# A fused RWKV and FFN kernel: a new order list, score tiles cleared on GpSimd, the last two stores in halves, and identity products around them

## The chip, the cores and the metric

The kernel runs on one core of a Trainium2 chip. The metric is device time in microseconds (us), the median of several runs; lower is better. The five instruction streams are TensorE (PE), VectorE (DVE), ScalarE (ACT), GpSimd (POOL) and SyncE (SP, which issues the DMAs).

## The reference

```python
# rwkv5: batch 4, 8 heads, 768 steps, head dimension 48
for t in range(S):
    cur = einsum('bhd,bhe->bhde', u[None] * kt, vt)
    y[:, :, t] = einsum('bhd,bhde->bhe', rt, state + cur)
    state = w[None, :, :, None] * state + einsum('bhd,bhe->bhde', kt, vt)
# bridge to x of 3072 x 384, then
h = (x @ w1) * (x @ w2) @ w3        # w1, w2: 384 x 1024, w3: 1024 x 1024
out = h @ w_out                     # w_out: 1024 x 384
```

The four FFN weights arrive as 64-bit words and are made into 32-bit numbers on the chip; all else is float32.

## The kernel before, in words

**The two halves.** The sequence is cut into six chunks of 128 steps, and each chunk into four batches; one chunk of one batch is a *unit*, numbered 0 to 23, so units 4c to 4c+3 are chunk c. For each unit the kernel loads k, r and v, scales k and r by powers of the decay, and gets from TensorE the inner sums for the running state, the scores of the unit, and the output rows. The output rows are turned into columns of `xT`, 512 tokens a chunk. The FFN then runs over whole chunks: products of `xT` with w1 and w2, multiplied together, and a last product with `w34`, which is w3 times w_out and is made once (`fold`, line 427, eight turns of 16 TensorE instructions). From chunk 1 on, both FFN products go by seven block products in place of eight, with sums of weights and of tokens.

**The weights.** There are 32 pieces, each through one of three `raw` buffers and one of two `t` buffers: 0 to 7 are strips of w1 and w2, 8 to 15 are w_out, 16 to 31 are w3. Piece i is loaded (SP), its magnitude is taken (ACT, line 385), its sign (POOL, line 396; DVE for pieces 0 and 1), the two are joined (DVE, line 401), its low word is scaled (ACT, line 405) and added (DVE, line 408). w3 is then turned (DVE, line 422) for the fold. A load waits for its `raw` buffer, and a sign waits for its `t` buffer.

**The order.** Nothing is scheduled when the kernel is built. `ORDER` is a list of some 1,430 words that an outside planner wrote, and `listed()` calls the step of each word in turn; each engine then runs its own steps in that order and waits by semaphores for what others make. A word is a letter and its indices. Those that matter here:

- SP: `kr.n`, `v.n` load unit n; `W.i` fetches weight piece i; `y.n`, `z.n` write a turned unit to DRAM and read it back; `D.c.m.x` stores rows (x = 1: `osb_top`, 0: `osb_low`), line 855.
- PE: `T.n`, `R.n` transposes of k and r (488); `U.n` inner sums (563); `A.n`, `Au.n` scores (570, 591); `S.n`, `V.n` output rows (690, 713); `yt.n` turns them (729); `a`, `b` the products of chunk 0 (759); `F.j` the fold (427); `pa`, `pb` the products of the later chunks (922, 926); `P.c.m.x` the seven last products (817); `Z.n.b` n products of the identity with itself (958), which nothing reads.
- DVE: `k.n` scaling (441); `i.n`, `j.n` state (609 to 615); `m.n`, `mo.n` scores into the tile `AT` under a mask (621, 595); `fe.n` a guard before V (702); `N`, `H`, `Q` steps of the weights (390, 401, 408); `G` turns w3 (422); `cz.i` clears one of two `AT` tiles (598).
- ACT: `t`, `r`, `ku` copies of turned k and r (495, 499, 585); `Y.n` takes output rows for units 0 to 4 (724), DVE later (722); `yx.n` puts them in `xT` (735); `M`, `L` steps of the weights (385, 405); `l.n` takes the read-back unit (527); `c` takes a product (765).
- POOL: `p.i` the sign of piece i (396); `vp.n` copies of v (697).
- `E.c.m.x` gathers the last products into output rows (DVE, lines 839 to 851; ACT for x = 0).

The scores of units 0 to 4 are taken differently from those of the others, which is why the two `AT` tiles are cleared once in between.

**The end.** In the list before, the last output tile is chunk 5, row block 0: `P.5.0.6` on TensorE, `E.5.0.7` on VectorE, and two stores of 128 rows by 384 columns (192 KB each). Each engine then leaves the fast arm of an If by a branch (line 1055) over the other arm's code, and drains (line 1084).

Of the kernel before, what the change touches and what calls it, by code (L numbers as in the profile page):

```python
# [23 lines left out]
v.1 kr.2 uw k.1 vs.0 ka.0 Z.4.0 T.1 kb.0 T.0 t.1 v.2 U.0 N.0 t.0 R.0 kr.3 ku.0 i.0 j.0 vp.1 U.1 R.1 i.1 r.0 j.1 r.1  # L24
A.0 kr.4 Au.0 k.2 M.0 S.1 S.0 ku.1 m.0 vp.2 R.2 T.2 mo.0 W.1 t.2 H.0 A.1 W.2 r.2 Au.1 fe.0 k.3 L.0 V.0 kr.5 Y.0 m.1
R.3 T.3 ku.2 mo.1 U.2 Q.0 A.2 t.3 Au.2 i.2 r.3 v.3 m.2 yt.0 M.1 mo.2 yx.0 fe.1 ku.3 k.4 Z.3.0 A.3 W.3 V.1 p.2 N.1 R.4
Y.1 v.4 H.1 T.4 M.2 S.2 j.2 kr.6 yt.1 L.1 Au.3 fe.2 H.2 V.2 yx.1 vp.3 Y.2 m.3 a.0.0.0 mo.3 L.2 W.4 yt.2 Q.1 M.3 U.3
W.5 i.3 p.3 t.4 Q.2 b.0.0.0 r.4 v.5 yx.2 k.5 ku.4 a.0.1.0 ub x.5 vp.4 c.0.0.0 A.4 H.3 c.0.1.0 S.3 y.5 ps fe.3 M.4 p.4
u.0.0.0 j.3 L.3 d.5 V.3 W.6 Q.3 M.5 U.4 v.6 Au.4 H.4 p.5 Y.3 kr.8 m.4 yt.3 L.4 b.0.1.0 mo.4 yx.3 i.4 vp.5 a.0.0.1 H.5
W.7 cz.1 a.0.3.2 L.5 Q.4 W.8 M.6 Q.5 p.6 c.0.0.1 vs.6 k.6 b.0.2.2 c.0.3.2 z.5 x.6 H.6 u.0.1.0 M.7 p.7 b.0.4.2 e.5 f.5  # L30
M.8 y.6 h.5 kr.7 L.6 j.4 H.7 S.4 W.9 U.5 L.7 fe.4 Q.6 V.4 l.5 Q.7 p.8 W.10 cz.0 Y.4 A.5 H.8 a.0.2.2 m.5 L.8 W.11 i.5
j.5 M.9 p.9 Q.8 b.0.3.2 k.7 c.0.2.2 z.6 H.9 M.10 p.10 u.0.2.2 L.9 Q.9 a.0.4.2 H.10 u.0.3.2 L.10 W.12 p.11 M.11 Q.10
x.7 a.0.1.1 c.0.4.2 H.11 W.13 L.11 u.0.4.2 U.6 l.6 Q.11 a.0.6.2 k.8 W.14 c.0.1.1 d.6 M.12 p.12 e.6 f.6 v.7 H.12
b.0.0.1 y.7 c.0.6.2 d.7 kr.9 p.13 M.13 e.7 L.12 b.0.1.1 f.7 H.13 Q.12 A.6 M.14 u.0.0.1 p.14 b.0.6.2 L.13 W.15 i.6 vs.7
Q.13 H.14 j.6 L.14 W.16 Q.14 a.0.5.2 u.0.6.2 m.6 W.17 x.8 M.15 p.15 u.0.1.1 a.0.7.2 c.0.5.2 d.8 e.8 z.7 H.15 M.16 p.16
# [12 lines left out]
s.0.0.3 B.3 pb.1.0.3 gb.1.0.5 E.0.1.2 P.0.0.2 gb.1.0.7 pa.1.1.0 E.0.0.2 E.0.0.3 P.0.0.1 ga.1.1.0 pa.1.1.1 E.0.0.1
pa.1.1.4 ga.1.1.5 P.0.0.6 pa.1.0.2 P.0.0.5 ga.1.0.6 gb.1.0.3 pa.1.1.5 E.0.0.6 E.0.0.7 pb.1.0.7 D.0.0.1 ga.1.1.1
pb.1.0.2 gb.1.0.4 gb.1.0.8 pa.1.1.6 gb.1.0.6 pb.1.1.0 ga.1.1.3 ga.1.1.2 s.1.0.0 pa.1.1.7 s.1.0.1 P.0.1.1 ga.1.1.4  # L50
s.1.0.3 pb.1.1.4 s.1.0.2 E.0.1.1 pa.1.1.2 P.0.0.4 ga.1.1.6 pa.1.1.3 E.0.0.4 E.0.0.5 D.0.0.0 S.8 ga.1.1.7 U.10 gb.1.1.0
fe.8 V.8 k.12 l.10 pb.1.1.5 v.11 x.12 z.11 A.10 gb.1.1.1 Y.8 pb.1.1.1 gb.1.1.3 i.10 m.10 pb.1.1.2 y.12 vs.11 kr.15
gb.1.1.5 j.10 P.1.0.0 gb.1.1.6 yt.8 E.1.0.0 P.0.1.5 yx.8 g.10 U.11 P.0.1.6 k.13 f.12 P.1.1.0 d.13 e.13 kr.16 x.13
pb.1.1.7 E.1.1.0 P.0.1.3 y.13 pb.1.1.6 E.0.1.3 E.0.1.6 E.0.1.7 P.0.1.4 gb.1.1.2 D.0.1.1 gb.1.1.4 pb.1.1.3 gb.1.1.8
s.1.1.0 s.1.1.1 P.1.0.5 gb.1.1.7 s.1.1.3 P.1.0.2 s.1.1.2 E.0.1.4 E.1.0.2 P.1.0.6 E.0.1.5 D.0.1.0 P.1.0.3 P.1.1.2
E.1.0.3 E.1.0.6 P.1.0.1 E.1.1.2 P.1.0.4 E.1.0.1 E.1.0.7 D.1.0.1 P.1.1.1 E.1.0.4 E.1.0.5 D.1.0.0 P.1.1.3 E.1.1.1 S.9
E.1.1.3 P.1.1.5 fe.9 l.11 z.12 V.9 E.1.1.6 A.11 Y.9 P.1.1.4 i.11 j.11 v.12 yt.9 m.11 P.1.1.6 yx.9 E.1.1.4 g.11 E.1.1.5
D.1.1.0 S.11 E.1.1.7 S.10 D.1.1.1 fe.11 V.11 fe.10 l.12 f.13 V.10 v.14 Y.11 U.12 v.13 vs.12 k.14 A.12 z.13 yt.11
pa.2.0.0 m.12 yx.11 Y.10 ga.2.0.0 i.12 yt.10 vs.14 pa.2.0.1 j.12 yx.10 x.14 g.12 U.13 xs.2.0 y.14 xs.2.1 S.12 xs.2.2
# [48 lines left out]
def kernel(  # L108
# [46 lines left out]
    DM = H * D  # L155
# [171 lines left out]
    def body(arm, fast):  # L327
# [269 lines left out]
        def clear(i):  # L597
            nc.vector.memset(ats[i], 0.0)
# [378 lines left out]
        def plain():  # L977
# [8 lines left out]
            def seven(c):  # L986
# [3 lines left out]
                for m in range(B // 2):  # L990
# [4 lines left out]
                    for x in range(2):  # L995
                        store(c, m, x, nc.scalar)
# [92 lines left out]
```

## Time and profile before

| what | us |
|---|---|
| median of 5 runs | 494.57 |
| lowest, highest | 493.32, 497.68 |
| the profiled execution, its own time | 495.46 |
| its span from first to last instruction | 493.6 |
| PE busy in the span | 472.7 |
| DVE busy | 329.3 |
| ACT busy | 197.5 |
| POOL busy | 63.3 |

The span is 1.9 us short of the execution's own time, and that execution is 0.9 us over the median. PE is busy for 96% of the span; matmuls overlap, so that share tells where PE stood still and not how fast it worked. Queue q1 carries the data, q8 and q14 carry instructions: q8 moved 42 packets of 16 KB and q14 blocks of 8 KB.

### The profile page before, as it was taken

How to read it: one execution, taken by the hardware profiler on the slowest of the kernel's cores; microseconds unless marked ns; L12 is line 12 of the kernel's file. 1: busy time of each engine (PE TensorE's matmuls, PEld its weight loads, DVE VectorE, ACT ScalarE, POOL GpSimd, SP SyncE). 2: the span in 40 equal slices, each digit the busy share in tenths (PEclk: the TensorE clock that was granted, in tenths of full speed). 3: DMA queues.
4: the chain of work that ended last, by engine and by line, in shares of the span. 5: the costliest groups of instructions: out<-in, count | busy, mean ns of one | idle time of the engine just before them, and what ended most of it. 6: DMA issues, size and time to landing. Idle time of an engine off the chain costs nothing.

```text
span 493.6 us, 12176 instructions
## 1 busy us (share of the span) xinstructions
PE 472.7 (96%) x5070; PEld 392.7 (80%) x5070; DVE 329.3 (67%) x647; ACT 197.5 (40%) x454; POOL 63.3 (13%) x57
## 2 busy tenths in 40 slices
PE   7699899989999999999999999999999999999995
PEld 6586454656769988997888898889998889888894
DVE  5689998989999257659685993677462536316152
ACT  4776555848622124028516362422263132122200
POOL 3047544354500000000000000000000000000000
PEclk9989999999999999999999999999999999999999
DMA  8989969999830004326524550044150000100002
GB/s 190 242 215 265 215 185 237 215 231 221 226 76 34 15 20 113 97 83 161 144 65 113 131 128 18 20 118 139 64 146 1 0 3 17 49 1 0 1 1 69
DMA packets 100479, 52.72 MB, mean 107 GB/s; under 512 B 79296, under 2 KB 89792, under 8 KB 100416
## 3 DMA queue, kind: packets, MB, share of 16 engines
q1 hardware_dynamic: 99792, 51.86, 40.6%
q8 instruction: 42, 0.69, 0.6%
q14 instruction: 21, 0.17, 0.1%
q10 hardware_dynamic: 624, 0.00, 0.1%
HBM read 39.65 MB, written 12.19 MB: 105 GB/s over the span
## 4 chain that ended last, share of the span: by engine, by line
PE 75%; DVE 13%; issue 3%; DMA 3%; POOL 2%; ACT 2%; SPq 1%; ACTq 0%; DVEq 0%; POOLq 0%
PE ps_accB L922 10%; PE ps_w L427 6%; PE ps_Ab L922 4%; PE ps_accC L922 3%; PE ps_accC L926 3%; PE ps_s4b L817 3%; PE ps_accB L926 3%; PE ps_a12b L817 3%; PE ps_Aa L922 3%; PE ps_a11b L817 3%; PE ps_s3t L817 3%; PE ps_s1t L817 3%; PE ps_a22t L817 3%; PE ps_s2t L817 3%; PE ps_Fb L926 2%
## 5 line engine op out<-in xcount | busy, mean ns | idle before, releaser
L396 POOL TENSOR_SCALAR t<-raw 128x512 f32<-128x512 f32 (+2 forms) x30 | 52.5, 1752 | 61.3 <-DMA raw<-in_moe_w_dram 18.2
L922 PE MATMUL ps_accB<-sumw,w 128*128 128x256 f32 x160 | 45.9, 389 | 0.0
L427 PE MATMUL ps_w<-wo,w3T 128*128 128x384 f32 x128 | 42.7, 488 | 0.1
L427 PEld LDWEIGHTS ps_w<-wo,w3T 128*128 128x128 f32 x128 | 23.9, 190 | 15.7 <-issue 0.4
L471 ACT ACTIVATE ynat<-vnat,dg 128x48 f32<-128x48 f32 x144 | 34.4, 324 | 0.5 <-PE ps_x L729 0.4
L922 PEld LDWEIGHTS ps_accB<-sumw,w 128*128 128x128 f32 x160 | 28.9, 190 | 6.0 <-ACT u2a L939 1.1
L735 ACT COPY xT<-ps_x 128x384 f32<-128x384 f32 x24 | 11.5, 481 | 54.5 <-PE ps_x L729 54.3
L405 ACT ACTIVATE t<-raw 128x512 uint32<-128x512 uint32 (+2 forms) x32 | 22.7, 710 | 19.8 <-DVE wo L401 8.7
L527 ACT COPY kT<-tt 128x1024 f32<-128x1024 f32 x19 | 19.9, 1046 | 25.0 <-PE ps_y L690 18.7
L441 DVE TENSOR_TENSOR krs<-krin,pn_in 128x768 f32<-128x768 f32 (+1 forms) x25 | 24.1, 969 | 5.7 <-PE ps_a L563 4.1
L922 PE MATMUL ps_accC<-xT,sumw 128*128 128x256 f32 x80 | 23.8, 379 | 0.0
L926 PE MATMUL ps_accB<-xT,w 128*128 128x256 f32 x80 | 23.8, 379 | 0.0
L926 PE MATMUL ps_accC<-xT,w 128*128 128x256 f32 x80 | 23.8, 379 | 0.0
L922 PE MATMUL ps_Ab<-xT,w 128*128 128x256 f32 x80 | 22.6, 384 | 0.4 <-ACT ps_accB L937 0.4
L759 PE MATMUL ps_a<-xT,w 128*128 128x512 f32 (+1 forms) x60 | 22.2, 514 | 0.8 <-ACT xT L735 0.8
L759 PE MATMUL ps_b<-xT,w 128*128 128x512 f32 (+1 forms) x60 | 22.2, 512 | 0.5 <-DVE half L609 0.5
L922 PE MATMUL ps_Aa<-xT,w 128*128 128x256 f32 x80 | 22.3, 381 | 0.4 <-ACT ps_accB L937 0.4
L922 PE MATMUL ps_accB<-sumw,sumw 128*128 128x256 f32 x80 | 20.7, 382 | 0.0
L621 DVE COPY_PREDICATED AT<-later,ps_a 128x512 f32<-128x512 int32 x24 | 17.6, 731 | 1.8 <-PE ps_a L591 1.4
L759 PEld LDWEIGHTS ps_a<-xT,w 128*128 128x128 f32 x60 | 11.1, 190 | 9.5 <-issue 7.2
L511 DVE STREAM_TRANSPOSE tr<-krs 128x768 f32<-128x768 f32 x19 | 18.4, 969 | 0.2
L759 PEld LDWEIGHTS ps_b<-xT,w 128*128 128x128 f32 x60 | 11.1, 190 | 9.3 <-issue 7.2
(187 smaller groups left out, 1091.3 us busy)
## 6 DMA issues: line engine op xcount, KB each, us to landing
raw<-in_moe_w_dram SPq DMA_DIRECT2D x64, 128.0 KB, 3.4
scratch<-tr SPq DMA_DIRECT2D x19, 384.0 KB, 3.4
raw<-in_moe_w_dram SPq DMA_DIRECT2D x8, 768.0 KB, 5.7
tt<-scratch SPq DMA_DIRECT2D x38, 128.0 KB, 2.8
krin<-in_k_dram SPq DMA_DIRECT2D x24, 192.0 KB, 3.7
krin<-in_r_dram SPq DMA_DIRECT2D x24, 192.0 KB, 4.2
vnat<-in_v_dram SPq DMA_DIRECT2D x24, 192.0 KB, 3.3
raw<-in_moe_w_out_dram SPq DMA_DIRECT2D x32, 96.0 KB, 2.8
```

Source lines behind the costliest of these rows:

```text
L396: nc.gpsimd.tensor_scalar(part["t", i].bitcast(F32), words(i)[1].bitcast(F32), 0.0, None, ALU.mult)
L405: nc.scalar.activation(out=part["t", i], in_=words(i)[0], func=COPY, scale=2.0 ** -29)
L427: nc.tensor.matmul(ps, lhsT=w3T[j][:, kc, :], rhs=wo[kc], start=(kc == 0), stop=(kc == KF - 1))
L441: nc.vector.tensor_mul(krs[n % NS][:, which, :, :D], kr[:, which], pn[:, which, :, :D])
L471: nc.scalar.activation(out=ynat[n][:, h, :], in_=vnat[n % NV][:, h, :], func=COPY, scale=dg[n][:, h:h + 1])
L511: nc.vector.transpose(out=blocks[n].rearrange("x m e t -> x e m t"), in_=krs[n % NS][:, :, :, :D])
L527: nc.scalar.copy(out=turned(n).rearrange("x g p (z t) -> x (g p) z t", t=Q), in_=tts.rearrange("x z e t -> x e z t"))
L621: nc.vector.copy_predicated(AT[n], later.bitcast(I32)[:, None, None, :].to_broadcast([C, 2, NP, T]), upper(n))
L759: nc.tensor.matmul(ps, lhsT=(w1 if x == "a" else w2)[:, z, q, js], rhs=xT[c][:, q, ts], start=(q == 0), stop=(q == KM - 1))
L817: nc.tensor.matmul(ps, lhsT=operand(c, j // 2, a)[:, j % 2, m * C:(m + 1) * C], rhs=w34[:, KH * (x == 1) + j, :DH] if x < 2 else made[b][: ...
L922: nc.tensor.matmul(ps, lhsT=quarter(w, g, i, x), rhs=(b11, b21, b22, t4, b12, t2, t3)[x], start=x in (0, 4) and i == 0, stop=True, skip_gr ...
L926: nc.tensor.matmul(ps, lhsT=wide_of[w][:, g + half * HZ, 2, i * P:(i + 1) * P], rhs=xT[c][:, 2, side * TH:(side + 1) * TH], start=False, s ...
```

## The change

It does four things.

1. **A new list**, planned again; the header of the change says that the plan takes account of TensorE's instruction packets. The same steps are called, but for those below. Among the moves: on SP `kr.4` goes ahead of `v.2` and `kr.3`; on DVE `Q.0` goes ahead of `k.3`; on PE `Au.1` goes behind `V.0`, `T.3` behind `Au.2`, `S.4` and `V.4` behind six products, and `U.9`, `A.9`, `pa.1.0.4` and other products go behind `F.7`. The weight pieces keep their order.
2. **`cz.1` and `cz.0`** run on POOL, between `p.6` and `p.7` and between `p.13` and `p.14`.
3. **The last two stores** (now of chunk 5, row block 1) become four of 192 columns, each issued when its half is made.
4. **Identity products**: `Z.3.0` (3) becomes `Z.7.1` (7, into another pool's tile, a little later), and a new `Z.4.0` (4) stands behind the last product of all.

```diff
 ORDER = """
-v.1 kr.2 uw k.1 vs.0 ka.0 Z.4.0 T.1 kb.0 T.0 t.1 v.2 U.0 N.0 t.0 R.0 kr.3 ku.0 i.0 j.0 vp.1 U.1 R.1 i.1 r.0 j.1 r.1
-A.0 kr.4 Au.0 k.2 M.0 S.1 S.0 ku.1 m.0 vp.2 R.2 T.2 mo.0 W.1 t.2 H.0 A.1 W.2 r.2 Au.1 fe.0 k.3 L.0 V.0 kr.5 Y.0 m.1
-R.3 T.3 ku.2 mo.1 U.2 Q.0 A.2 t.3 Au.2 i.2 r.3 v.3 m.2 yt.0 M.1 mo.2 yx.0 fe.1 ku.3 k.4 Z.3.0 A.3 W.3 V.1 p.2 N.1 R.4
-Y.1 v.4 H.1 T.4 M.2 S.2 j.2 kr.6 yt.1 L.1 Au.3 fe.2 H.2 V.2 yx.1 vp.3 Y.2 m.3 a.0.0.0 mo.3 L.2 W.4 yt.2 Q.1 M.3 U.3
...
-d.11 L.28 y.10 F.5 e.11 W.31 Q.28 M.29 p.29 G.6.0 f.11 kr.12 H.29 M.30 p.30 v.10 L.29 Q.29 H.30 pa.1.0.1 z.10 X.5
-G.6.1 p.31 L.30 M.31 Q.30 F.6 ga.1.0.5 G.7.0 xs.1.0 E.0.0.0 xs.1.1 xs.1.2 kr.13 vs.10 H.31 s.0.1.0 L.31 Q.31 s.0.1.1
-xs.1.3 U.9 wa.0 X.6 A.9 wa.1 pa.1.0.4 wa.2 pa.1.0.5 G.7.1 wa.3 F.7 ga.1.0.1 wb.0 ga.1.0.3 wb.2 k.11 s.0.1.2 kr.14 i.9
...
-E.5.1.4 P.5.1.5 P.5.0.3 E.5.1.5 E.5.1.6 D.5.1.0 E.5.1.7 D.5.1.1 P.5.0.1 E.5.0.3 P.5.0.5 E.5.0.4 P.5.0.6 E.5.0.6
-E.5.0.1 E.5.0.5 D.5.0.0 E.5.0.7 D.5.0.1
+v.1 kr.2 uw k.1 vs.0 ka.0 Z.4.0 T.1 kb.0 T.0 kr.4 t.1 U.0 N.0 t.0 R.0 ku.0 i.0 j.0 vp.1 U.1 v.2 R.1 r.0 i.1 j.1 r.1
+A.0 kr.3 k.2 Au.0 M.0 S.1 S.0 m.0 ku.1 R.2 mo.0 W.1 T.2 H.0 t.2 A.1 W.2 r.2 vp.2 fe.0 L.0 kr.5 Q.0 V.0 k.3 Au.1 Y.0
+R.3 m.1 ku.2 v.3 U.2 mo.1 fe.1 M.1 N.1 A.2 k.4 Au.2 W.3 T.3 M.2 p.2 m.2 V.1 kr.6 mo.2 t.3 r.3 i.2 R.4 H.1 Y.1 T.4 A.3
+ku.3 v.4 H.2 vp.3 j.2 L.1 d.5 W.4 L.2 Q.1 Z.7.1 yt.0 M.3 W.5 Q.2 S.2 p.3 Au.3 yx.0 fe.2 kr.7 yt.1 t.4 m.3 V.2 yx.1
+mo.3 r.4 a.0.0.0 vp.4 H.3 Y.2 ku.4 U.3 v.5 A.4 p.4 i.3 L.3 yt.2 k.5 b.0.0.0 yx.2 Q.3 M.4 W.6 x.5 b.0.1.0 M.5 p.5 kr.8
+H.4 c.0.0.0 ps j.3 L.4 u.0.0.0 y.5 H.5 vp.5 S.3 a.0.1.0 fe.3 L.5 Q.4 W.7 Q.5 M.6 p.6 V.3 W.8 Au.4 Y.3 m.4 c.0.1.0 yt.3
+U.4 mo.4 yx.3 cz.1 v.6 k.6 a.0.0.1 z.5 x.6 U.5 c.0.0.1 H.6 b.0.4.2 M.7 p.7 i.4 L.6 j.4 M.8 k.7 y.6 vs.6 W.9 a.0.2.2
...
+Q.30 z.10 L.31 s.0.1.0 vs.10 Q.31 F.6 ga.1.0.5 s.0.1.1 G.7.0 wa.0 wa.1 G.7.1 wa.3 wb.0 F.7 xs.1.0 E.0.0.0 X.6 xs.1.1
...
+D.5.1.1.0 P.5.1.5 E.5.1.4 D.5.1.0.0 P.5.1.6 Z.4.0 E.5.1.6 E.5.1.5 D.5.1.0.1 E.5.1.7 D.5.1.1.1
 """
...
         def clear(i):
-            nc.vector.memset(ats[i], 0.0)
+            nc.gpsimd.memset(ats[i], 0.0)
...
-        def store(c, m, x, queue=nc.sync):
+        def store(c, m, x, part=None, queue=nc.sync):
             row = (m if x else B // 2 + m) * S + c * C
-            queue.dma_start(out=out[row:row + C, :], in_=made["top" if x else "low", c, m])
+            cols = slice(0, DM) if part is None else slice(part * DH, part * DH + DH)
+            queue.dma_start(out=out[row:row + C, cols], in_=made["top" if x else "low", c, m][:, cols])
```

`busy_array(times, at)`, which a word `Z` calls, takes a tile of 128 columns from one of two PSUM pools and issues `times` products of the 128 x 128 identity with itself into it; its text is not changed. In the plain arm the call of `store` names its queue by keyword, with no other effect.

## The prediction

> **What bounds the kernel.** I read the page first, then busy time by stage, then the chain that ended last, then the end of the trace record by record.
>
> ```profile
> span 493.6 us, 12176 instructions
> PE 472.7 (96%) x5070; PEld 392.7 (80%) x5070; DVE 329.3 (67%) x647; ACT 197.5 (40%) x454; POOL 63.3 (13%) x57
> PE   7699899989999999999999999999999999999995
> DVE  5689998989999257659685993677462536316152
> DMA  8989969999830004326524550044150000100002
> ```
>
> PE is full from the sixth slice to the last. DVE and the DMA engines are full too, but only in the first third, while the weights are made. The stages, as start:end, length, busy time of PE, PEld, DVE, ACT, POOL, granted clock, DMA share, GB/s:
>
> ```profile
> 20.47:24.12 3.65, 0.00 (x1) 0.00 (x0) 0.83 (x1) 2.18 (x5) 0.00 (x0) 1.00 1.08 314
> 60.00:90.00 30.00, 30.00 (x234) 16.17 (x233) 28.07 (x54) 18.56 (x39) 14.70 (x10) 1.00 0.79 208
> 90.00:142.08 52.08, 50.45 (x447) 33.19 (x446) 48.55 (x84) 32.60 (x73) 21.57 (x13) 1.00 0.87 207
> 142.08:300.00 157.92, 156.41 (x1778) 137.49 (x1778) 112.20 (x224) 61.17 (x155) 0.00 (x0) 1.00 0.35 90
> 300.00:487.65 187.65, 186.55 (x1660) 167.46 (x1658) 92.29 (x188) 49.23 (x113) 0.00 (x0) 1.00 0.13 39
> ```
>
> After 142.08 PE stands for 1.5 + 1.1 = 2.6 us in 345: nothing there can give much. What a list can win lies before 60 us, in the weights up to 142, and behind PE's last product at 487.65. Three places of the chain (start, length, what):
>
> ```profile
> 20.47 3.65 issue
> ...
> 107.74 5.16 PE ps_w L427 x16
> ...
> 142.08 5.21 PE ps_w L427 x16
> ```
>
> The first is PE waiting for nothing the profile shows. The trace's q8 records explain it: each packet of 16 KB stands for 128 weight loads with 128 matmuls, so q8 is PE's own code; the block due here starts only at 21.74 and takes 0.96, amid data that keep the DMA engines over 100% busy. The clock then falls to 0.5 from 24.6 to 28.0. The folds of the other two lines are just in time: the turns of w3 that feed them (line 422) end at 106.48 and 141.74.
>
> **Part 1, the list: up to 60 us.** I walked both lists by hand with the durations of the trace. The stall stays: as many PE instructions, less four, stand before it, the load on the queues is the same, and moving `kr.4` ahead swaps equal transfers of 192 KB. `Q.0` (0.95) ahead of `k.3` delays `R.3` to 21.3 and `U.2` to 21.8 (before 19.05 and 20.04), inside the stall, so it costs nothing; without the stall it would cost 1.8. Behind it, `a.0.0.0` waits for `yx.1`, now behind `L.1`, `L.2`, `M.3` (0.92 each), `yx.0` and `t.4` on ACT: 34.1 where it was 32.56. `a.0.0.1` waits for `yx.3` in both: 45.16 before, some 45.5 now. So PE is level there, or 1 us late. The weights are not: the sign of piece 5 waits for `Q.3` to free a `t` buffer, 42.9 before; with H and L of pieces 1 to 3 pulled forward, `Q.3` ends near 38.3 and `Q.5` near 44.3 (before 49.2). DVE work ahead of `Q.5`, summed step by step from the rows, falls from 32.3 to 29.6, so it runs 2.2 us ahead of its old lag as well. Then PE stood three times between 53.9 and 59: 0.78 (`S.4`, for the state), 0.61 (`V.4`, for the guard), 1.15 (`A.5`, for ACT's copy of the read-back unit), 2.5 in all. Now six products of 1.3 to 2.7 us, ready by the earlier pieces, stand before `S.4`, and `A.5` comes 10 us behind the copy. I count these 2.5 us as won at 60 us, less the 0.4 above: 2.1.
>
> **Up to the last fold.** PE work ahead of `F.7`, summed the same way, falls from 113.6 to 110.5 us; DVE work ahead of the last turn, `G.7.1`, from 116.3 to 111.5. PE began `F.7` at 142.08, a lag of 28.5. DVE began `G.7.1` at 141.04; less 4.8 and the 2.2 won it begins near 134 and ends at 134.7. PE, with 2.1 us won and one visit more to the small products from `a.0.0.0` to `F.7` (12 for 11, 0.3 us, priced below), would be there at 142.08 - 3.1 - 1.8 = 137.2, so it need not wait. As the work ahead is 3.1 less, the gain is **1.8 us**. On the way some waits change place: those of 0.89, 0.80 and 0.45 from 103.6 to 107 (`S.7`, `V.7`, `yt.7`) go, but `V.7` now stands before `F.1` while its guard stands behind `G.1.1`, `Y.6`, `f.8` and `Q.20` on DVE (1.9 us), and `F.3` comes up with little before it. I set these equal. What could take it is DMA: the last piece landed at 132.8, and from there to the turn's end took 8.9; it must land near 127. DMA was only 79% busy from 60 to 90, for lack of free buffers, so 6 us lie there. Bounds: a gain of 4 (the waits near 104 go and none comes) and a loss of 3.1 (rival D).
>
> **After it.** PE's steps are the same in number; 26 visits to small products in place of 25. A visit of 32 instructions between large products costs 0.81 us and one of 64 costs 1.29 (start to start, less the products), so 0.33 per visit: **+0.3**. The waits of 0.3 to 0.8 that I find in the start times add to 3.9; the new list has as many places where a turn or a `Y` stands close before its user. I take 0, bounds -3 and +3.
>
> **Part 2, clearing.** DVE loses two steps of 0.48. POOL's own clears of the same tile took 0.54. `cz.1` waits for `V.3` (near 43) and has `p.7` behind it, whose piece lands later; `cz.0` waits for `V.4` with `p.14` behind it. POOL was idle 61.3 us before its signs. Its gain is in DVE's sum above; own cost 0, bounds 0 and +1.1 if a sign is late by both.
>
> **Parts 3 and 4, the end.** The last three steps, SP's longest wait, and the DMA queues from 490.1 to 491.4 (packets, MB, share):
>
> ```profile
> 487.45 0.33 SPq L855 DMA_DIRECT2D out_dram<-osb_low  x1
> 487.69 0.36 DVE L851 TENSOR_TENSOR osb_top<-ps_s4b,u 128x192 f32<-128x192 f32 x1 [0.27 <-PE ps_s4b L817]
> 488.08 0.33 SPq L855 DMA_DIRECT2D out_dram<-osb_top  x1
> ```
>
> ```profile
> SPq L1084 <- DMA out_dram<-osb_top: 2.9, 1, 2.9
> ```
>
> ```profile
> q8 instruction: 1, 0.02, 4.6%
> q1 hardware_dynamic: 4, 0.00, 2.0%
> ```
>
> Fourteen of the store's 16 parts landed by 489.94, in 1.9 us, the median of all 12 such stores; one came at 490.63, the last at 492.46. Its few packets moved only after a block of PE code (490.18, 0.95 us) and beside one of q14 (491.46). PE had fetched code at 484.41, at 485.58 and at 490.18: I read them as an ordinary block entered a few instructions before the program's end, the branch's target, and the block behind it once PE had drained (488.5). Now the four added products of `Z.7.1` and the four of `Z.4.0` are 32 instructions more behind the same block start, and PE ends 8 x 0.11 = 0.9 us later. The ordinary block is then fetched some 1.7 us earlier against the last product, the target during that product, and the one behind it near 491, when the stores have landed. The next limit is VectorE's closing drain at 490.87, behind its own fetch; SP's wait ended at 492.50. Gain 1.6, and 0.1 from halves (same 128 rows, half the bytes): **1.7 us**. Bounds: 2.0; and -0.9 if the fetch still hits a store and PE's longer end is what is waited for. `Z.7.1` costs 0.9 more than `Z.3.0`, and lies before `a.0.0.0`, where PE waits 0.9 for `yx.1`.
>
> The Trainium skill, "Runtime: NRT & Kernel Launch", section "Instruction fetch mechanics", says that code is refilled in 16 KiB blocks of 256 instructions and that crossing into one is mostly hidden. The packets agree (128 pairs), the 3.65 us at 20.47 do not; by the page this part would be worth 0 and the sum -1.5.
>
> **Sum.** -1.8 + 0.3 + 0 + 0 - 1.7 = -3.2, against the profiled execution's 495.46: 492.3. That execution is 0.9 over the median of 494.57, from which the same sum gives 491.4. Between the two I say **491.8**.
>
> **Rivals.** From the middle of those two bases, 495.0:
> - A, forecast: 490.3 to 493.3. Chance 0.47.
> - B, only the end improves: the weights are bound by DMA bytes, which are the same, and the early lead is spent before `F.7`. For it: DMA is 0.98 busy from 100 to 120. 495.0 - 1.7 = 493.3. Chance 0.17.
> - C, both larger: 495.0 - 4 - 2.0 + 0.3 = 489.3. Chance 0.14.
> - D, slower: `F.7` was pulled forward by 3.1 us of PE work, and the last turn does not come earlier than 141.7. PE, in order, then waits at `F.7` with that work behind it: 495.0 + 3.1 + 0.3 = 498.4 (if the end is won as well, 496.7). It decides when the last piece lands after 129. For it: the fold was just in time already. Against: DVE has 4.8 us less to do before the turn. Chance 0.14.
> - E, the moves cancel, and the fetch lands on another store: 495. Chance 0.08.
>
> Within 0.5% (492.1 to 497.0) is about what a measurement of this kernel can't tell from no change. Of A 0.34 lies under 492.1 and 0.13 above; C is faster; B and E are the same; of D 0.01 is the same and 0.13 slower. So faster 0.48, same 0.39, slower 0.13. The range 488.8 to 497.0 leaves out some 0.05 of C and most of D.
>
> **What would show it.** PE idle of some 3.6 us near 21 again; no wait over 0.5 us from 50 to 60; `F.7` between 135.5 and 138.5 with no wait before it; SP's last wait for a store under 1.5 us with q8 quiet between the last store and its landing. I am wrong if `F.7` starts after 139, or if waits after it add to over 6 us.

## The result, and the profile after

The changed kernel takes 495.55 us (median of 52 runs, 493.71 to 497.67). Over all the runs beside which the kernel before was measured its own median is 496.95 (94 runs), so the five runs shown above lay low. The ratio is **0.9973, 95% interval 0.9963 to 0.9984**: 1.3 us faster, where 3.2 (0.9935) was forecast. The sign is right, the size is less than half.

The profiled execution after has a span of 492.1 us. The page, the same rows as before:

```profile
span 492.1 us, 12219 instructions
PE 477.9 (97%) x5086; PEld 395.5 (80%) x5086; DVE 326.7 (66%) x645; ACT 197.8 (40%) x454; POOL 64.1 (13%) x59
PE   7799999899999999999999999999999999999997
DVE  5779799999887377668875894389554436324352
DMA  8999768898900042435625261025240000100002
```

TensorE is no less full than before, and 5.2 us busier (its 16 added matmul instructions, and a granted clock of 0.5 from 22.7 to 29.6 us, where before it was 0.5 from 24.6 to 28.0, are in that). Busy time by stage, cut where the new list has its folds (start:end, length, PE, PEld, DVE, ACT, POOL, granted clock, DMA share, GB/s):

```profile
17.68:21.35 3.67, 1.45 (x86) 1.31 (x77) 2.15 (x5) 3.26 (x9) 0.59 (x2) 1.00 0.99 327
21.35:23.51 2.16, 1.00 (x20) 0.71 (x20) 2.06 (x4) 0.92 (x1) 0.00 (x0) 0.82 1.11 325
60.00:90.00 30.00, 28.73 (x321) 16.14 (x321) 27.84 (x55) 16.39 (x31) 13.97 (x10) 1.00 0.81 218
90.00:138.75 48.75, 47.71 (x371) 30.04 (x370) 43.79 (x74) 33.38 (x80) 22.26 (x13) 1.00 0.90 210
138.75:300.00 161.25, 160.69 (x1854) 140.44 (x1852) 115.56 (x231) 61.95 (x156) 0.00 (x0) 1.00 0.34 87
300.00:488.41 188.41, 187.76 (x1667) 168.68 (x1666) 92.74 (x188) 49.06 (x113) 0.00 (x0) 1.00 0.14 41
```

The lost time near 21 is still there, cut in two. From 60 to 90, where TensorE was full before (30.00), it now stands for 1.3 us. `F.7` starts at 138.75 (141.91 before, by its first product), and the last product ends at 488.41 (487.65). The waits of SyncE for the last stores (us in total, times, longest), and the DMA queues from 490.9 to 492.2:

```profile
SPq L1086 <- DMA out_dram<-osb_low: 0.5, 2, 0.3
SPq L1086 <- DMA out_dram<-osb_top: 0.5, 1, 0.5
```

```profile
q8 instruction: 1, 0.02, 5.5%
q14 instruction: 1, 0.01, 1.7%
```

The wait of 2.9 us is gone, and behind 490.9 the queues carry code only: the last part of a store landed at 490.84, the fetch of TensorE's code began at 491.14. Between the two profiles the span falls by 1.5 us, which divides like this:

| stretch | before | after | change | forecast |
|---|---|---|---|---|
| start to `F.7` | 141.91 | 138.75 | -3.2 | -4.9 |
| `F.7` to the end of the last product | 345.74 | 349.66 | +3.9 | +3.1 + 0.3 |
| end of the last product to the end of the span | 5.96 | 3.71 | -2.2 | -1.7 |

In this pair the end gave what was forecast and the list nothing. But this is one execution of each, and the experiments show that the first stretch moves by up to 3.2 us between executions of the same list.

### The profile page after: what moved, and what is told of

Same layout as the page of the kernel before. It is cut to its first block, busy times and chain, and to the rows that moved or that the text cites. A ratio compares the mean times of both kernels' runs of the same rounds, so it can differ in the third digit from the quotient of the medians.

```text
span 492.1 us, 12219 instructions
## 1 busy us (share of the span) xinstructions
PE 477.9 (97%) x5086; PEld 395.5 (80%) x5086; DVE 326.7 (66%) x645; ACT 197.8 (40%) x454; POOL 64.1 (13%) x59
## 4 chain that ended last, share of the span: by engine, by line
PE 79%; DVE 9%; DMA 3%; ACT 3%; issue 1%; SPq 1%; POOL 1%; ACTq 0%; DVEq 0%; POOLq 0%
PE ps_accB L924 11%; PE ps_w L427 5%; PE ps_Aa L924 4%; PE ps_Ab L924 4%; PE ps_accC L924 4%; PE ps_accB L928 4%; PE ps_accC L928 4%; PE ps_s2t L817 3%; PE ps_a22t L817 3%; PE ps_a11b L817 3%; PE ps_s1t L817 3%; PE ps_s3t L817 3%; PE ps_s4b L817 3%; PE ps_a12b L817 3%; DMA raw<-in_moe_w_dram 2%; PE ps_y L690 2%
## 5 line engine op out<-in xcount | busy, mean ns | idle before, releaser
L396 POOL TENSOR_SCALAR t<-raw 128x512 f32<-128x512 f32 (+2 forms) x30 | 53.2, 1773 | 55.8 <-DMA raw<-in_moe_w_dram 22.8
L924 PE MATMUL ps_Aa<-xT,w 128*128 128x256 f32 x80 | 22.7, 386 | 0.4 <-ACT ps_accB L939 0.4
L943 DVE TENSOR_TENSOR ps_accC<-ps_Fb,u2b 128x512 f32<-128x512 f32 x10 | 7.0, 699 | 20.3 <-ACT u2b L941 18.9
```

The lines of the kernel that those rows point to most:

```text
L396: nc.gpsimd.tensor_scalar(part["t", i].bitcast(F32), words(i)[1].bitcast(F32), 0.0, None, ALU.mult)
L924: nc.tensor.matmul(ps, lhsT=quarter(w, g, i, x), rhs=(b11, b21, b22, t4, b12, t2, t3)[x], start=x in (0, 4) and i == 0, stop=True, skip_gr ...
```

## The experiments

All ratios are to the kernel before, measured beside it. "F.7", "last" (end of the last product that is read, the identity products left out), "end" (from there to the end of the span) and "strip 7" (landing of the last strip of w1 and w2) are from the one profile of each kernel, in us. All 18 runs, and the two kernels of the case:

| kernel | ratio, 95% interval | strip 7 | F.7 | last | end |
|---|---|---|---|---|---|
| before | 1 | 51.0 | 141.91 | 487.65 | 5.96 |
| after | 0.9973 (0.9963 to 0.9984) | 51.0 | 138.75 | 488.41 | 3.71 |
| e1: old list, new end | 0.9957 (0.9935 to 0.9980) | 54.2 | 143.75 | 489.81 | 4.00 |
| e2: new list, old end | 1.0002 (0.9982 to 1.0022) | 52.8 | 141.97 | 491.84 | 3.96 |
| e3: old list, four products last | 0.9970 (0.9941 to 0.9998) | 51.6 | 142.29 | 487.77 | 4.39 |
| e4: after, three early products | 0.9980 (0.9958 to 1.0003) | 53.1 | 141.97 | 491.83 | 3.80 |
| e5: after, no products last | 1.0022 (0.9996 to 1.0047) | 53.2 | 140.53 | 490.70 | 4.39 |
| e6: old list, halves only | 0.9993 (0.9970 to 1.0016) | 53.6 | 143.48 | 489.08 | 5.53 |
| e7: old list, seven early products | 1.0014 (0.9987 to 1.0041) | 54.0 | 143.98 | 489.49 | 5.46 |
| e8: after, clears on VectorE | 0.9988 (0.9970 to 1.0006) | 51.3 | 139.41 | 489.16 | 3.82 |
| e9: after, small steps first | 1.0006 (0.9978 to 1.0035) | 52.5 | 140.69 | 490.27 | 3.75 |
| e10: e1, guard first | 0.9943 (0.9919 to 0.9967) | 55.4 | 145.95 | 491.77 | 3.74 |
| e11: after, half loads | 0.9880 (0.9850 to 0.9911) | 49.6 | 136.24 | 486.39 | 3.98 |
| e12: e1, half loads | 0.9929 (0.9908 to 0.9950) | 51.8 | 143.24 | 489.29 | 5.69 |
| e13: after, two loads back | 0.9986 (0.9962 to 1.0010) | 46.6 | 140.17 | 490.16 | 3.75 |
| e14: e1, two loads forward | 1.0039 (1.0012 to 1.0066) | 56.0 | 145.87 | 491.35 | 6.41 |
| e15: e13 and e9 together | 0.9983 (0.9959 to 1.0007) | 47.9 | 140.22 | 489.83 | 3.91 |
| e16: e13, three loads back | 0.9975 (0.9949 to 1.0001) | 46.1 | 140.30 | 490.39 | 3.82 |
| e17: e1, one load back | 0.9937 (0.9910 to 0.9964) | 49.0 | 141.74 | 487.38 | 3.78 |
| e18: e17 and e10 together | 0.9953 (0.9931 to 0.9975) | 48.4 | 141.73 | 487.29 | 3.94 |

### The end and the list apart

e1 puts the new end on the old list, with the changed `store`:

```diff
-P.5.0.5 E.5.0.4 P.5.0.6 E.5.0.6 E.5.0.1 E.5.0.5 D.5.0.0 E.5.0.7 D.5.0.1
+P.5.0.5 E.5.0.4 D.5.0.0.0 P.5.0.6 E.5.0.6 E.5.0.1 D.5.0.1.0 E.5.0.5 D.5.0.0.1 E.5.0.7 D.5.0.1.1 Z.4.0
```

> The old list with the new end alone: the two last stores in column halves and the four identity products last. Theory M (read from the two profiles: from the last product's end to the span's end 5.96 us before and 3.71 after, so the end is worth -2.25, while the list itself brought the last product 0.75 later): ratio to the kernel before 0.9955, -2.2 us. Rival N (the prediction's split: list -1.5, end -1.7, and the profile of the changed kernel caught a slow pass through the list): -1.7, 0.9966. Rival O (the end is worth nothing on most executions, the late landing of the profile of before was one of its kind): 1.000 to 1.002, the 0.9 us of added products included.

e2 takes the new end off the new list:

```diff
-P.5.1.4 E.5.1.3 D.5.1.1.0 P.5.1.5 E.5.1.4 D.5.1.0.0 P.5.1.6 Z.4.0 E.5.1.6 E.5.1.5 D.5.1.0.1 E.5.1.7 D.5.1.1.1
+P.5.1.4 E.5.1.3 P.5.1.5 E.5.1.4 P.5.1.6 E.5.1.6 E.5.1.5 D.5.1.0 E.5.1.7 D.5.1.1
```

> The new list and the clearing on GpSimd, with the old end: whole stores, no identity products last. Theory M: the list alone is 0.75 us slower, ratio 1.0015. Rival N: the list alone is 1.5 us faster, 0.997. Rival O: the whole gain is the list's, 0.9973.

e1 gave 0.9957 and e2 1.0002. The end carries the whole gain, 2.1 us with 1.1 either way; the list, with the clears on GpSimd and the seven early products, costs 0.1 us with 1.0 either way, and the forecast 1.5 us of gain (0.997) lies outside the interval. This bears out theory M.

### What of the end it is

e3 adds the one word `Z.4.0` to the old list, e6 only the halves, e5 takes only `Z.4.0` out of the changed kernel:

```diff
 e3
-E.5.0.1 E.5.0.5 D.5.0.0 E.5.0.7 D.5.0.1
+E.5.0.1 E.5.0.5 D.5.0.0 E.5.0.7 D.5.0.1 Z.4.0
 e6
-P.5.0.5 E.5.0.4 P.5.0.6 E.5.0.6 E.5.0.1 E.5.0.5 D.5.0.0 E.5.0.7 D.5.0.1
+P.5.0.5 E.5.0.4 D.5.0.0.0 P.5.0.6 E.5.0.6 E.5.0.1 D.5.0.1.0 E.5.0.5 D.5.0.0.1 E.5.0.7 D.5.0.1.1
 e5
-P.5.1.6 Z.4.0 E.5.1.6
+P.5.1.6 E.5.1.6
```

> The old list and whole stores, with four identity products at the end: the one edit. If they carry the whole gain of the end (halves alone gave 0.9993, both 0.9957, leaving them out of the changed kernel 1.0022): 0.9950 to 0.9970, the span ending 3.7 to 4.2 us behind the last product, and the last fetch of TensorE's code 2.6 us or more behind it. If halves are needed with them: 0.998 to 1.000.

> The old list with the two last stores in halves and nothing else. If the halves carry the gain: 0.9955 to 0.997. If the identity products carry it: 0.9995 to 1.001, with the span ending 5.5 to 6 us behind the last product as before.

> The changed kernel without the four identity products at the end; the column halves stay. If the identity products carry the gain of the end (the prediction: they bring the fetch of TensorE's code behind the last product forward): the end goes back to 5 us or more behind the last product, ratio 0.9995 to 1.001. If the halves carry it, or the end of the new list is short by where its code blocks fall: 0.996 to 0.9975, 0.9 us of products less.

The products without halves gave 0.9970, the halves without products 0.9993, and the changed kernel without the products 1.0022 (0.9973 with them). So it is the products; for the halves no gain could be told. (In their one profile the end is 4.39 in both e3, where 3.7 to 4.2 was expected, and e5, where 5 or more was; the ratios go by all the runs.) SyncE's waits for the last stores in e5 and e6 say how:

```profile
SPq L1085 <- DMA out_dram<-osb_top: 2.1, 1, 2.1
```

```profile
SPq L1085 <- DMA out_dram<-osb_low: 1.2, 1, 1.2
SPq L1085 <- DMA out_dram<-osb_top: 0.6, 2, 0.4
```

In e5 the last fetch of TensorE's code runs from 491.90 to 493.05, 1.2 us behind the last product, and one part of the last store lands at 494.06, where the other fifteen were there by 493.15. Over all 20 profiles, that fetch starts 1.2 to 2.5 us behind the last product without the four products, and 2.5 to 3.3 with them, when the store has mostly landed; the two groups touch, in before and e11. The last part of the last store is 0.9 us or more late behind the one before it in four of five kernels without the products (before, e5, e6, e7) and in two of fifteen with them (e12, e14); and in all six it lands 1.0 to 1.4 us after the end of that fetch. So the products do not exclude it, they make it rare. SyncE's waits of e14 (fetch 494.64 to 495.65, last part at 496.73) look like those of before:

```profile
SPq L1085 <- DMA out_dram<-osb_top: 2.8, 2, 2.6
```

That the fetch holds the part up is read from the times of both, and the earlier stores bear it out. The 20 profiles have 512 stores of output rows. In 156 of them such a fetch began before 14 of the store's 16 parts had landed and ended over 0.6 us behind the store's issue: the last part came over 0.8 us behind the fourteenth in 108 of these, and in 14 of the other 356. The block of q14 that the prediction saw beside the late part is no regular company: in e5 it starts at 494.20, behind the landing.

The Trainium skill, "Runtime: NRT & Kernel Launch", section "Instruction fetch mechanics", has the crossing into a new block mostly hidden. Here sixteen instructions more, whose results nothing reads, made 1.5 us (e3, with 1.4 either way): on this reading such a fetch is not hidden at the program's end.

### The early identity products

e4 has three in the new list, e7 seven in the old one:

```diff
 e4
-L.2 Q.1 Z.7.1 yt.0 M.3
+L.2 Q.1 Z.3.1 yt.0 M.3
 e7
-ku.3 k.4 Z.3.0 A.3 W.3
+ku.3 k.4 Z.7.1 A.3 W.3
```

> The changed kernel with three early identity products in place of seven (eight passes of 0.11 us less). Theory M: the four added products are not hidden and the last product ends 0.9 us sooner, ratio 0.9955 where the changed kernel has 0.9973. The prediction's step (hidden by the wait before the first product of the weights): no change, 0.9973. If their use is to shift the blocks of TensorE's code by 16 instructions, it gets slower, 0.998 or above, by a late block at another place.

> The old list with seven early identity products in place of three. The prediction's step (hidden by the wait before the first product of the weights, which is 0.9 us in the old list): no change, 1.000. Theory M: 0.9 us dearer or, in the old list, in part hidden, 1.000 to 1.002. If the shift of the code blocks by 16 instructions helps the end by itself: 0.9970.

e4 was no faster than the changed kernel (0.9980), and in e7 `a.0.0.0` starts at 32.04, where the four other kernels with that list and three products (before, e1, e3, e6) have 31.53 to 32.84. With three products in the new list, TensorE waits for `yx.1` before `a.0.0.0`; in the changed kernel it does not. From PE's waits of e4, 30 to 60 us:

```profile
PE ps_a L758 <- ACT xT L734: 0.6, 1, 0.6
```

So the 0.9 us is mostly or wholly hidden, as the prediction had it, and theory M was wrong in this. The third case of e4's expectation (0.998 or above, by a late block elsewhere) can't be told apart from no change.

### Where the list's gain went

PE's waits from 30 to 60 us (us in total, times, longest). The changed kernel, then e2, the same list:

```profile
PE ps_a L759 <- ACT a L765: 1.1, 1, 1.1
PE ps_x L729 <- ACT ynat L724: 0.4, 1, 0.4
PE ps_y L690 <- DVE st L614: 0.2, 1, 0.2
```

```profile
PE ps_x L728 <- ACT ynat L723: 2.3, 1, 2.3
PE ps_y L689 <- ACT a L764: 1.9, 1, 1.9
PE ps_y L712 <- DVE AT L701: 0.2, 1, 0.2
```

The three waits of the old list (`S.4`, `V.4`, `A.5`) are gone, but `S.3` (`ps_y`, at 41 us) and `yt.3` (`ps_x`, at 47) wait instead: 1.9 + 2.5 us of lost time in e2, 1.6 + 2.5 in e4, 1.0 + 1.7 in e5, and 0.4 + 0.6 in the profile of the changed kernel, the mildest of these four. There the first of the lines above, 1.1 us at 57.4, comes on top. In e2, VectorE's and then ScalarE's steps around them (start, us, engine, line, what, idle time before it and its cause):

```profile
39.73 0.96 DVE L400 SCALAR_TENSOR_TENSOR w<-w,t 128x768 uint32<-128x768 uint32 x1 [1.20 <-POOL t L395]
40.60 0.35 DVE L613 TENSOR_TENSOR st<-ps_u,half 128x192 f32<-128x192 f32 x1
40.99 0.65 DVE L614 TENSOR_TENSOR st<-st,wn_in 128x192 f32<-128x192 f32 x1
```

```profile
40.12 0.90 ACT L384 ACTIVATE w<-raw 128x768 f32<-128x768 f32 x1 [2.32 <-DMA raw<-in_moe_w_dram]
40.93 0.35 ACT L764 COPY a<-ps_a 128x256 f32<-128x256 f32 x1
...
46.10 0.90 ACT L384 ACTIVATE w<-raw 128x768 f32<-128x768 f32 x1 [1.42 <-DMA raw<-in_moe_w_dram]
46.90 0.52 ACT L723 COPY ynat<-ps_y 128x192 f32<-128x192 f32 x2
```

The steps that TensorE needs are short: the state (`st`), the take of a product (`a`), the take of output rows (`ynat`). Each stands behind a weight step that waits: the copies on ScalarE behind one for a strip (strip 5 landed at 40.1 and strip 6 at 46.1), the state on VectorE behind one for a sign on GpSimd. The old list has the same fault one strip later: in e1 strip 7 lands at 54.2, `H.7` waits for it, the guard `fe.4` stands behind `H.7`, and `V.4` loses 2.5 us where the profile of before, with strip 7 at 51.0, shows 0.6. PE's longest wait of e1 from 30 to 60 us:

```profile
PE ps_y L713 <- DVE AT L702: 2.9, 2, 2.3
```

A wait can also cost more than its own length here. Behind the wait for `yt.3` in e2, from 47.2 to 54.0 us, the granted clock (third number from the end) shows 0.5, and a product of 512 columns at 53.2 is followed by the next after 0.91 us, where it is 0.43 at the full clock:

```profile
40.00:50.00 10.00, 6.15 (x123) 4.86 (x124) 6.98 (x11) 4.96 (x9) 7.41 (x5) 0.86 0.95 260
50.00:60.00 10.00, 10.00 (x53) 5.39 (x52) 7.70 (x12) 4.95 (x8) 3.38 (x2) 0.80 0.96 192
```

`F.7` comes 3.2 us later in e2 than in the changed kernel. PE's waits from 17 us to `F.7` add up to 9.0 us and 7.4, and the clock stands at 0.5 for 10.2 us and 6.9, which by an estimate (half of the 3.3) is 1.7 us of work more; together 3.3. In e13 (below) the clock is 0.5 from 72.3 to 75.7, behind a wait of 2.0 us. That the wait brings the fall is read from the times alone: behind e5's wait of 1.4 us at 47.5 there is none.

e9 moves the small steps of the new list ahead, e10 the guard of the old one (on top of e1):

```diff
-b.0.1.0 M.5 p.5 kr.8 H.4 c.0.0.0 ps j.3 L.4 u.0.0.0 y.5 H.5 vp.5 S.3 a.0.1.0 fe.3 L.5 Q.4 W.7 Q.5 M.6 p.6 V.3
+b.0.1.0 kr.8 j.3 c.0.0.0 M.5 p.5 H.4 ps L.4 u.0.0.0 y.5 vp.5 S.3 a.0.1.0 fe.3 H.5 L.5 Q.4 W.7 Q.5 p.6 V.3
...
-yx.3 cz.1
+yx.3 M.6 cz.1
```

```diff
-L.6 j.4 H.7 S.4 W.9 U.5 L.7 fe.4 Q.6 V.4 l.5 Q.7
+L.6 j.4 S.4 W.9 U.5 fe.4 H.7 Q.6 V.4 l.5 L.7 Q.7
```

> The changed kernel with four steps that wait for a strip of the weights (M.5, p.5, H.4, H.5 and M.6) moved behind the small steps for which TensorE waits (c.0.0.0, j.3, fe.3 and Y.3 with yx.3): the same work and the same transfers. Theory Q (in the new list TensorE stands at S.3 and at yt.3, 1.1 us in its own profile but 4.4 and 4.1 in the profiles of the two variants, since those small steps queue behind weight steps that wait for a strip to land): these waits fall under 1 us and the time by 1 to 3 us against the changed kernel, ratio to the kernel before 0.992 to 0.995. Rival R (the strips' bytes bound all that leads to the last fold): the waits go, others of the same sum come before the last fold, ratio 0.997 as for the changed kernel.

> The old list with the new end, and with H.7 moved behind the guard fe.4 and l.5 ahead of L.7. Theory Q: the old list's waits between 53 and 60 us (2.5 us in the profile of before, 4.1 and 4.7 in two others) are of the same kind, the guard standing behind H.7, which waits for strip 7; they fall by 2 us or more, ratio 0.990 to 0.993 where the same kernel without the move has 0.9957. Rival R: the waits move to a later place, 0.9957.

Neither helped beyond the noise (1.0006 against 0.9973; 0.9943 against 0.9957). In e9 the wait at `S.3` went, the one at `yt.3` stayed (1.4 us), and new ones came up, the largest later. PE's waits of e9 from 30 to 60 us:

```profile
PE ps_a L758 <- ACT a L764: 2.7, 1, 2.7
PE ps_x L728 <- ACT ynat L723: 1.4, 1, 1.4
PE ps_a L758 <- DVE abt L767: 1.0, 1, 1.0
```

The 2.7 us lie at 59.4, so rival R held: theory Q's waits were real, but taking them out did not move the time.

### Bytes, and the order of the loads

e11 and e12 leave out the loads of four of the eight heads for units 3 to 9:

```diff
-                queue.dma_start(out=dst, in_=src[b, :, ts, :].rearrange("h t d -> t h d"))
+                hs = H // 2 if 3 <= n <= 9 else H
+                queue.dma_start(out=dst[:, :hs], in_=src[b, :hs, ts, :].rearrange("h t d -> t h d"))
```

> The changed kernel, but of units 3 to 9 only four of the eight heads of k, r and v are loaded (the other four keep what an earlier unit left, so this part of the input is left out): 288 KB less for each unit, all steps and their order the same. Rival R, now my theory (the strips land at the same times under both lists, piece 5 near 40 us and piece 7 near 53, because the DMA engines are full from 10 to 60 us, and the small steps queue behind them): piece 7 lands 3 us or more earlier, the waits from 41 to 48 us fall under 1.5 in all, the last fold starts 3 us or more earlier (137 or before), time 0.988 to 0.992 of the kernel before. If it is ACT and DVE that bound the first part: strips land earlier but the last fold within 1 us, 0.996 to 0.998.

> The old list with the new end and the same loads left out as in the run before. Theory R: the waits from 53 to 60 us fall under 1.5 in all and the last fold starts 2 us or more earlier than 143.5; ratio 0.986 to 0.991 where the same kernel with all loads has 0.9957. If the new list was worth its 1.5 us wherever strips are not late, this one stays 1.5 us behind the run before it in this list.

Here the lists part. The new one takes 0.9880 (four runs) and the old one 0.9929 (ten), and `F.7` starts at 136.24 against 143.24; the last product ends 2.9 us sooner (486.39, 489.29). PE's waits of e11 from 30 to 60 us are one line, and the DMA share (second number from the end) leaves room, where e2 has 0.92 and 0.96 in the first and last of these stretches:

```profile
PE ps_x L730 <- ACT ynat L725: 0.4, 1, 0.4
```

```profile
30.00:40.00 10.00, 10.00 (x217) 8.57 (x216) 8.13 (x14) 8.97 (x19) 7.04 (x5) 1.00 0.71 204
40.00:50.00 10.00, 9.48 (x169) 6.61 (x168) 9.77 (x16) 5.19 (x11) 6.65 (x6) 1.00 0.96 268
50.00:60.00 10.00, 10.00 (x55) 4.54 (x54) 8.99 (x13) 7.21 (x13) 5.34 (x4) 1.00 0.64 185
```

So with half of these loads the new list is worth what was forecast, and more, and the bytes of the unit loads take it away. (e12's end of 5.69 had a late part, so some of the difference of the ratios may be the end's; the 2.9 us are before it.) For the old list theory R failed: its `F.7` moved by 0.5 us from e1's 143.75, not by 2 or more.

The new list also issues unit loads sooner, which the prediction had noticed of `kr.4` alone: `kr.7` at 31.9 us where it was 52.2, and `kr.8` at 39.6 where it was 43.2. e13 moves both back, e16 `kr.6` as well, e15 joins e13 with e9's edit, and e14 does the opposite to e1. In SP's order of the loads:

```diff
 e13
-W.5 kr.7 v.5 W.6 kr.8 W.7 W.8 v.6 W.9
+W.5 v.5 W.6 W.7 kr.7 W.8 v.6 W.9 kr.8
 e16, besides
-kr.6 v.4 W.4 W.5
+v.4 W.4 W.5 kr.6
 e14
-W.5 v.5 W.6 v.6 kr.8 W.7 W.8 kr.7 W.9
+W.5 kr.7 v.5 W.6 kr.8 v.6 W.7 W.8 W.9
```

> The changed kernel with the load of unit 7 moved behind strip 7 and that of unit 8 behind strip 9; the same bytes in all. Theory S (the order of the transfers: 768 KB of unit loads, 3 us at the 260 GB/s moved from 40 to 50 us, stand ahead of strip 7 without need): strip 7 lands by 51 us, the waits from 41 to 60 us fall under 2 us, the last fold starts at 139 or before, 0.992 to 0.995. Rival T (the sum of bytes up to 60 us decides, whatever their order): 0.997 to 0.998 as for the changed kernel.

> The old list with the new end, and the loads of units 7 and 8 ahead of strips 6 and 7 as the new list has them. Theory S: strip 7 lands later by the 384 KB of unit 7, 1 to 1.5 us, and the time rises by as much, 0.998 to 0.999 where the same kernel without the move has 0.9957. Rival T: 0.9957, no change.

> As e13, with the small steps ahead of the weight steps as well (e9's edit, which alone gave 1.0006). Theory S: no worse than e13 and up to 1 us better, 0.990 to 0.994. Rival T: 0.997 or above.

> As e13, with the load of unit 6 behind strip 5 too (it stood ahead of strip 4). Theory S: strips 4 and 5 land 1 to 1.5 us sooner, the wait at S.3 near 41 us falls under 0.5 us, 0.990 to 0.994; if unit 6 then lands too late for its own scaling (49 us in the list), 0.995 or above with a new wait after 50 us. Rival T: 0.997.

In e13 strip 7 landed at 46.6, 4.4 us or more sooner than in the changed kernel and before it did in e11 (49.6), and PE's waits from 30 to 60 us were 1.1 and 0.4, where the changed kernel's profile has 1.7 in all and e2's 4.4. The time did not fall (0.9986; e15 0.9983, e16 0.9975), so it is not the landing of strip 7 alone that decides. PE's waits of e13 from 30 to 120 us, and ScalarE at the first:

```profile
PE ps_a L758 <- ACT a L764: 2.0, 1, 2.0
PE ps_w L426 <- ACT t L404: 1.2, 1, 1.2
PE ps_y L689 <- DVE st L613: 1.1, 1, 1.1
```

```profile
70.75 0.55 ACT L384 ACTIVATE wo<-raw 128x384 f32<-128x384 f32 x1 [3.23 <-DMA raw<-in_moe_w_out_dram]
71.20 0.53 ACT L404 ACTIVATE t<-raw 128x384 uint32<-128x384 uint32 x1
71.64 0.57 ACT L764 COPY a<-ps_a 128x512 f32<-128x512 f32 x1
```

The same picture 25 us later: the take stands behind a piece of w_out that has not landed, and `F.3` then loses 1.3 us at 114.9 behind its own piece. With all its bytes, each wait taken out of the new list was followed by another further on. Rival T's number held for it, though the order did change when the strips landed. `F.7` is 3.9 us later in e13 than in e11: the waits from 17 us on make 2.1 of that (7.8 against 5.7), the clock at 0.5 behind the wait of 2.0 us another 1.7 by the same estimate. For the old list theory S held, in sign at least: e14 is 1.0039 where e1 is 0.9957, strip 7 at 56.0, PE's largest wait 3.0 us. The 4 us are more than the 1 to 1.5 expected. In the two profiles the spans differ by 3.9 us: `F.7` comes 2.1 later, the stretch behind it is 0.6 shorter, and the end, with its late part, is 2.4 longer.

e17 and e18 ask what room the old list has, on e1 and on e10:

```diff
-v.6 kr.8 W.7 W.8 kr.7 W.9
+v.6 W.7 W.8 kr.7 kr.8 W.9
```

> The old list with the new end, and the load of unit 8 behind that of unit 7, so behind strips 7 and 8. If the order of the transfers sets the first part of the old list: strip 7 lands 1 to 1.5 us sooner, the waits from 53 to 60 us stay at their 2.5 us or below, 0.992 to 0.994 where the same kernel without the move has 0.9957. If the old list is at its own limit (VectorE) when strips are in time: 0.9950 to 0.9965.

> As e17, with the guard ahead of strip 7's step and the row copy ahead of its low half (e10's edit, 0.9943). If both count: 0.990 to 0.993. If the weights' chain further on takes it back: 0.9943 to 0.996.

e17 gave 0.9937, strip 7 at 49.0, and one wait of 0.6 us from 50 to 60, with one of 2.1 us before it, at 42.6 (`yt.3`); e18 0.9953, the second of its two cases. Old list, new end and a later `kr.8` make the lowest median of the study with all loads (493.18 us, beside 496.55 for the kernel before), but the intervals of e1, e10, e17 and e18 overlap, so which of the four is best is not told.

### The clears

e8 puts `cz` back on VectorE:

```diff
-            nc.gpsimd.memset(ats[i], 0.0)
+            nc.vector.memset(ats[i], 0.0)
```

> The changed kernel with the two clears on VectorE again, at the same places of the list. The prediction's step (its 0.96 us on VectorE lies in the lead up to the last turn, which has slack of 1.1 us at the last fold but 0.1 to 0.2 at the fourth): 0 to 1 us slower than the changed kernel, 0.9973 to 0.9993. Rival (the clears on GpSimd delay a sign of 2.8 us): up to 1 us faster, 0.9953.

0.9988, with the changed kernel at 0.9973: the forecast's direction, but within the noise.

## Why the prediction was wrong

- **The end (-1.7): right.** e1 measured 2.1 us, and the products carry it in the way named, as far as the times show: the fetch behind the last product comes later against the store, and seldom meets it; SyncE's last wait came to 0.5 us, under the 1.5 named. Of the 32 instructions that were counted, the 16 of `Z.4.0` do it alone (e3); those of `Z.7.1` give nothing alone (e7). The 0.1 for the halves can't be told from nothing (e6: 0.9993).
- **The list (-1.8 + 0.3): failed.** It measured +0.1 us (e2). The step that failed is "I count these 2.5 us as won at 60 us, less the 0.4 above: 2.1". The three waits did go, as said. In their place `S.3` and `yt.3` waited 1.0 to 4.4 us in the four profiles above, with 1.1 more at 57.4 in the changed kernel's. The walk used each row's duration and each buffer's release, and put no price on weight steps pulled forward. They did come forward: the pair of low words that ends with `Q.5` ended at 44.9 in the changed kernel's profile (44.3 forecast) and 45.9 in e2. But pulling the weight steps forward put them, on engines that run their steps in order, ahead of steps that TensorE waits for, while the strips landed little sooner: strip 5 at 38.5 to 40.7 and strip 6 at 43.5 to 46.6 in the six profiles of the new list with its loads in place (after, e2, e4, e5, e8, e9), 39.8 to 41.6 and 45.3 to 47.1 in five of the old (before, e1, e3, e6, e7). The granted clock behind a wait had no term either.
- **The transfers: passed over.** "moving `kr.4` ahead swaps equal transfers of 192 KB" was all that was said; `kr.7` moved by 20 us, ahead of strips 6 and 7. By e13 that delays strip 7 by 4.4 us or more in the new list; by e13's time, putting it right is not enough.
- **Which rival came true:** B, "only the end improves: the weights are bound by DMA bytes", priced at 493.3 of 495.0, or 0.9966; measured 0.9973. Its reason, the early lead spent for the bytes, is borne out by e11. It had 0.17; its row ("DMA is 0.98 busy from 100 to 120") stood in the text, but the queues full in 20 to 60 us were not weighed against strips wanted 4 us sooner.
- **`F.7`: 137.2 was forecast,** with no wait before it; 138.75 came in the profile of the changed kernel and 139.4 to 142.0 in e2, e4, e5 and e8. With half loads it was 136.24: the walk was right for transfers that do not hold the steps up. That nothing waits right before it was right, and rival D's wait never came, though its sign did: the last piece landed at 130.1, after 129, and the last turn ended at 137.72, 1.0 us ahead of `F.7`. The sign "no wait over 0.5 us from 50 to 60" failed (1.1).
- **Behind `F.7`: +3.4 forecast,** +3.9 measured, and the same within 0.6 in every profile of either list (345.5 to 346.1, 349.6 to 350.2). The nearness is partly luck: the waits there, whose change was taken as 0, fell from 2.6 us to 1.2 by the windows, so TensorE's work behind `F.7` grew by some 5.3 us, not 3.4; by which products is open.
- **Near 21 us:** `R.3` was put at 21.3 and came at 21.35. The stall is 3.8 us in all as before, now 2.4 before `R.3`, behind `k.3`, and 1.4 in `U.2`.
- **The identity products ahead (0): right** (e4, e7). **The clears (0 to 1.1): open** (e8).
- **The base.** Five of the old list's profiles have `F.7` at 141.9 to 144.0, that of before being the earliest, with strip 7 at 51.0 where the others have 51.6 to 54.2. Its waits from 53 to 60 us, 2.5 where e1 and e7 have 4.1 and 4.7, were among the shortest that list shows.

What stays open: which link of the weights' chain (landing, SyncE's issues, the steps of the pieces) makes the waits of the new list between 60 us and `F.3`, near 115, once strip 7 is early. Behind `F.3` it is none: from its start to that of `F.7` TensorE takes 25.3 us in all ten profiles of the new list, and 28.0 to 28.3 in all ten of the old.

## What to carry to other kernels

Before a step is moved forward in an in-order queue, look at what it waits for: if that is a transfer, and the DMA engines are already full, everything behind the step inherits the landing time, and the wait only changes its name. Check each load that a new list moves against the transfers it now stands ahead of, not the first one alone. Look at the granted clock behind each long wait as well: here, by the estimate, it cost e2 as much again as its longer waits. And take the base from several profiles where a stage hangs on transfers: its waits differ by 2 to 3 us from one execution to the next, as much as the whole change was forecast to be worth.

## What the runs showed of the hardware

The block of TensorE's code that the stall near 21 waits for was fetched anywhere from 18.3 us (e3) to 21.7 (before) in the old list with all its loads, and at 22.2 in e12. With 18.3 the stall in `U.2` was 0.5 us and not 3.9, and yet `a.0.0.0` started only 1.0 us sooner (31.53, before 32.56), and `F.0` not at all (91.15, before 91.11): `V.1`, for one, then waited 1.7 us at 26. Halving the unit loads did not make the stall shorter (4.4 us in e12, with a DMA share of 0.57 from 20 to 30), so full DMA engines, which the prediction named, are not its whole cause.
